# Sliding attention with a gated MLP on one core: values ahead of scores in one unit, gates, sums and applies in another order, and an end with all products copied by ScalarE

## The chip, the cores and the metric

The kernel runs on one core of one Trainium2 chip. The metric is the device time of one execution in microseconds (us). Three timed runs of the kernel before took 201.37, 201.47 and 202.03 us, with a median of 201.47.

## The reference: what is computed

```python
xn = _layernorm(x)                       # x: 1 x 2048 x 512, bf16
s  = _A_ref(xn, A_wqkv, A_wo)            # attention, then @ wo
g  = _silu(_B_ref(xn, w1, w2, w3, w4))   # MLP
return x + s * g
```

`_A_ref` is attention with 32 heads of 16 columns. Each position looks at 8 positions: itself and those 2, 4, ... 14 before it; positions before the start are masked. The softmax runs over these 8. `_B_ref` normalises, multiplies by `w1` (512x512), takes gelu, shifts the four quarters of the columns by -1, +1, -2 and +2 positions, multiplies by `w2`, adds its input, normalises again, and runs an MLP through 1376 columns (`w3`, gelu, `w4`) that is added as well.

## The kernel before

The 2048 positions are split into even and odd ones (`p` = 0, 1; 1024 each), since the attention only couples positions of the same parity. Everything is issued in an order written out by hand: `pin` keeps each instruction in program order on its engine, so each of TensorE (PE), VectorE (DVE), ScalarE (ACT) and SyncE (SP, which issues nearly all DMAs) works through its own list and waits at its head. Nothing is rescheduled.

**First part (until about 113 us).** Normalisation, q, k, v, `w1`, `w2`, and `w3` with gelu for four chunks of 512 positions. The results of `w3` stay in SBUF as `h3a` and `h3b`. The change touches nothing here.

**Second part: 18 units** (`for n in range(NU)`, line 843). A unit is 114 positions of one parity, in two blocks of 57. Units 0 to 8 are even positions, 9 to 17 odd ones. In unit `n` TensorE's list holds:

- `scores(n)` (line 584): 32 small matmuls of q against k into PSUM banks 0 to 3, then one exponential on ScalarE over 128x1824 elements (line 598), which writes the tile `prob`.
- `band(n - 1)` (line 600): VectorE zeroes by a minimum with a mask (line 603) what lies outside the 8 positions. From unit 15 on the band is that of unit `n` itself and stands later in the unit.
- `values(n - 2)` (line 608): 32 small matmuls of `prob` with v into bank 4 (`O_ps`, line 617) and 16 with `den_st` or `den_s2` into bank 5 for the softmax's denominators (`D_ps`, line 627); then ScalarE copies bank 4 into `oT` (line 632). From unit 16 on it is `values(n - 1)`, and unit 15 does both 13 and 14.
- a share of the 16 `w4` groups (`w4_take`, line 828; the matmuls are on line 729). A group is 128 positions and 11 matmuls; it holds one of a few free banks, and when its last matmul is issued, `done` puts the sum with the input on VectorE (line 742), which empties the bank, and appends a tanh for ScalarE (`tanhs`, line 749) and behind it a gate for VectorE (`gates`, line 751). For the tiles 13 to 15 the silu itself is taken on ScalarE (lines 745 and 740), without a gate. Tile 15 adds its input by an identity matmul (line 734).
- a small extra group: v for the odd positions in units 0 to 7 (`g_v`, line 758), and from unit 8 on one output tile (`g_fin`, line 770): four matmuls with `wo` (line 776), a copy on ScalarE (line 786), and, appended to `finals`, the multiply by the gate (line 790) and the sum with x (line 796) on VectorE. `stores` holds the writes to HBM.

The denominators are turned over in batches of units (0 to 3, 4 to 7, 8 to 11, 12 to 15, and 16 with 17). In units 5, 9, 13 and 16 (`ends`), `inverse` takes the reciprocal on VectorE (line 639), `write_rec` writes it to HBM by two DMAs on SyncE (line 648), one unit later `read_rec` reads it back spread over the heads (line 651), and two units after the reciprocal, or behind the loop for the fourth batch, `apply` multiplies `oT` by it on VectorE (line 664).

What stands where within a unit is set by the lines 851 to 893: the lists `finals`, `gates` and `tanhs` are emptied (`flush`) at fixed places between the three thirds of the unit's `w4` share.

**The end (lines 895 to 921).** `values(17)`, the last reciprocal, the last 8 matmuls of `w4`; then `expand` (line 666) spreads the last reciprocal over the heads by 8 matmuls into two banks, `keep_ps` copies them to SBUF on ScalarE (line 678, the "kept factors" `rk`), and `apply_kept` multiplies them into `oT` (line 684). Seven output tiles of the odd positions remain. Tiles 1 to 5 are copied by ScalarE; for tile 6 and the two halves of tile 7 VectorE multiplies straight out of PSUM (`act=False`, line 792). Tiles 1 to 5 are stored by SyncE, tile 6 and the first half of 7 by ScalarE's queue, and the second half by SyncE.

Of the kernel before, what the change touches and what calls it, by code (L numbers as in the profile page):

```python
# [20 lines left out]
def kernel(  # L21
# [17 lines left out]
    PE, DVE, ACT, POOL, SP = nc.tensor, nc.vector, nc.scalar, nc.gpsimd, nc.sync  # L39

    def pin(ins):

        return tc.keep_in_program_order(ins)
# [3 lines left out]
    D = 512  # L47
# [37 lines left out]
    def b4(shape, name):  # L85
        return sm4.tile(shape, BF16, name=name, tag="b4")
# [121 lines left out]
    class Norm:  # L208
# [22 lines left out]
        def apply(self, lo, hi):  # L231
            for j in range(lo, hi):
                pin(DVE.tensor_scalar(
                    out=self.dst[:, j, :], in0=self.src[:, j, :], scalar1=self.mv[:, j, 0:1],
                    scalar2=self.rstd[:, j : j + 1], op0=ALU.subtract, op1=ALU.mult,
                ))
# [347 lines left out]
    def scores(n):  # L584
        p, u = n // UP, n % UP
        for dt in range(ND):
            for k in range(2):
                b = 2 * u + k
                for rg in range(4):
                    r = slice(32 * rg, 32 * rg + 32)  # L590
                    pin(PE.matmul(  # L591
                        S_ps[:, rg, (2 * dt + k) * QB : (2 * dt + k + 1) * QB],
                        lhsT=kM[p][r, dt, b * QB + 1 : b * QB + 65, :].rearrange("p k e -> p (k e)"),
                        rhs=qT[p][r, dt, b * QB : (b + 1) * QB], start=True, stop=True,
                        tile_position=(32 * rg, 0),
                    ))
        pr = probs[n] = b4([P, 4, ND * NQ], "prob")
        pin(ACT.activation(pr, S_ps[:, :, 0 : ND * NQ], AF.Exp, scale=SCALE))  # L598

    def band(n):  # L600
        pr = probs[n]
        f = pr.rearrange("p r x -> p (r x)")
        pin(DVE.tensor_tensor(out=f, in0=f, in1=maskb[:], op=ALU.min))  # L603
        if n % UP == 0:
            z = pr[0:14].rearrange("p r (a k q) -> p (r a) k q", k=2, q=QB)
            pin(DVE.memset(z[:, :, 0, 0:7], 0.0))

    def values(n):
        p, u = n // UP, n % UP
        if u == 0:  # L610
            oT[p] = b8([P, ND, MQ], f"oT{p}")
        pr = probs.pop(n)
        for dt in range(ND):
            for k in range(2):
                for rg in range(4):
                    x = (2 * dt + k) * QB
                    pin(PE.matmul(  # L617
                        O_ps[32 * rg : 32 * rg + 32, x : x + QB],
                        lhsT=va_r[:, n % NV, k, 32 * (4 * dt + rg) : 32 * (4 * dt + rg) + 32],
                        rhs=pr[:, rg, x : x + QB], start=True, stop=True, tile_position=(0, 32 * rg),  # L620
                    ))
        b = batch_of[n]
        lo, hi = batches[b]
        st = den_st if hi - lo == 4 else den_s2
        for dt in range(ND):
            for rg in range(4):
                pin(PE.matmul(  # L627
                    D_ps[32 * rg : 32 * rg + 32, :], lhsT=st[:, 4 * (n - lo) + dt, :],
                    rhs=pr[:, rg, dt * NQ : (dt + 1) * NQ], start=(n == lo and dt == 0),
                    stop=(n == hi - 1 and dt == ND - 1), tile_position=(0, 32 * rg),  # L630
                ))
        pin(ACT.activation(
            oT[p][:, :, u * NQ : (u + 1) * NQ], O_ps[:, 0 : ND * NQ].rearrange("p (a q) -> p a q", q=NQ), AF.Copy
        ))
# [15 lines left out]
    def read_rec(b):  # L650
        pin(SP.dma_start(
            out=rr_t.rearrange("p j a q -> p (j a q)"),
            in_=ap_of(rec_ds[b][:], [[16 * NQ, 16], [0, 8], [1, 16 * NQ]]),
        ))
# [42 lines left out]
    tanhs, gates, vstores = [], [], []  # L697
# [72 lines left out]
    def g_fin(p, i, st=None, n=2, half=False, act=True, cols=None, later=None):  # L770

        c = slice(0, D) if cols is None else slice(*cols)
        W = c.stop - c.start

        def one(pt, dt):
            pin(PE.matmul(  # L776
                pt[:, 0:W], lhsT=oT[p][:, dt, i * P : (i + 1) * P], rhs=wo["sb"][:, dt, c],
                start=(dt == 0), stop=(dt == ND - 1),
            ))

        def done(pt):
            sg = fin.tile([P, D], BF16, name="sg", tag="f")[:, 0:W]
            pt = pt[:, 0:W]
            g = xn[p][:, i, c]
            if act:
                pin(ACT.activation(sg, pt, AF.Copy, scale=2.0 if half else 1.0))  # L786

            def steps():
                if act:
                    pin(DVE.tensor_tensor(out=sg, in0=sg, in1=g, op=ALU.mult))  # L790
                elif half:
                    pin(DVE.scalar_tensor_tensor(out=sg, in0=pt, scalar=2.0, in1=g, op0=ALU.mult, op1=ALU.mult))
                else:
                    pin(DVE.tensor_tensor(out=sg, in0=pt, in1=g, op=ALU.mult))
                x_o = xo[p][:, i, c]
                pin(DVE.tensor_tensor(out=x_o, in0=sg, in1=x_o, op=ALU.add))
                if cols is not None:
                    pin(st.dma_start(out=ov[p, i * P : (i + 1) * P, c], in_=x_o))
                elif st is not None:
                    stores.append((now["n"], lambda: store(st, p, i + 1 - n, n)))  # L800

            if later is None:
                steps()
            else:
                later.append(steps)

        return Group(ND, one, done)

    finals = []
# [8 lines left out]
    def flush(q):  # L818
        while q:
            q.pop(0)()  # L820

    def flush_stores(n):
        while stores and stores[0][0] <= n:
            stores.pop(0)[1]()
# [3 lines left out]
    def w4_take(k, extra=()):  # L828

        while k > 0 and open_w4:  # L830
            k -= open_w4[0].take(k)
            if open_w4[0].at == open_w4[0].n:
                open_w4.pop(0)
                if extra:
                    extra.pop(0).all()
# [5 lines left out]
    ends = {5: 0, 9: 1, 13: 2, 16: 3}  # L841
    load_va(0)
    for n in range(NU):
        now["n"] = n
        q = W4 * (n + 1) // NU - given
        given += q
        extra = small_g.get(n, [])
        if n == 0:
            w4_take(HEAD)

        if n - 1 in ends:
            read_rec(ends[n - 1])
        scores(n)
        if 1 <= n < 16:
            band(n - 1)
        if n >= 2:
            values(n - 2 if n < 16 else n - 1)
        if n + 1 < NU:
            load_va(n + 1)
        if n in xo_at:  # L860
            load_xo(*xo_at[n])
        if n == 4:
            load_wo()
        if n - 1 not in ends:
            flush_stores(n - 2)
        flush(vstores)
        flush(finals)
        if n in ends:
            recs[ends[n]] = inverse()
            write_rec(ends[n])  # L870
        if n == 17:
            free += [2, 3]
            pin(ACT.preload_act_table_set("silu_and_others"))
        w4_take(q // 3)
        if n < 15:
            flush(gates)
        flush(tanhs)
        if n == 15:
            apply(ends[n - 2])
        if n == 17:  # L880
            band(n)
        w4_take(q // 3, extra)
        if n < 15 and n - 2 in ends:
            apply(ends[n - 2])
        if 15 <= n < 17:
            band(n)
        if n == 15:
            values(14)
        w4_take(q - 2 * (q // 3), extra)
        if n >= 15:  # L890
            flush(gates)
        while extra:
            extra.pop(0).all()

    n = NU
# [4 lines left out]
    flush(gates)  # L900
    flush(tanhs)
    w4_take(LAST)
    banks = [PS[:, i, :] for i in range(2)]
    for j in range(2):
        expand(rec, NU - 2 + j, banks[j])
    kept = [keep_ps(b) for b in banks]
    flush(finals)
    g_fin(1, 1, SP).all()
    flush(tanhs)
    for j in range(2):  # L910
        apply_kept(NU - 2 + j, kept[j])
    g_fin(1, 2).all()
    g_fin(1, 3, SP).all()
    flush_stores(n)
    g_fin(1, 4).all()
    g_fin(1, 5, SP, half=True).all()
    flush_stores(n)
    g_fin(1, 6, ACT, 1, half=True, act=False).all()
    flush_stores(n)
    g_fin(1, 7, ACT, half=True, act=False, cols=(0, D // 2)).all()  # L920
    g_fin(1, 7, SP, half=True, act=False, cols=(D // 2, D)).all()


# [28 lines left out]
```

## Time and profile before

| | |
|---|---|
| timed runs, median | 201.47 us |
| the profiled execution, own time | 201.1 us |
| its span, first to last instruction | 199.3 us |
| TensorE matmul busy | 189.3 us (95%) |
| ScalarE busy | 128.5 us (64%) |
| VectorE busy | 117.9 us (59%) |
| GpSimd busy | 19.4 us (10%) |
| DMA, mean | 142 GB/s |
| granted TensorE clock, mean | 0.993 |

All durations come from the one profiled execution, whose own time is 1.8 us more than its span. In the timeline a line gives the start, the duration, the engine, the line of the kernel, the operation with what it writes and reads, and in brackets how long the engine had idled just before and what ended that. In the list of waits a line gives who waited for whom, with the total, the number of times and the longest. The chain of waits is followed back from the last instruction.

### The profile page before, as it was taken

Reading aid. Unit: us, or ns where it says so; the run is one execution under the profiler, and the core shown is the slowest. Engines: PE = TensorE matmul, PEld = TensorE weight load, DVE = VectorE, ACT = ScalarE, POOL = GpSimd, SP = SyncE. Lnnn points to the kernel's source line nnn. Section 1 sums busy time; section 2 is a strip of 40 time slices with the busy share of each in tenths; the row PEclk is TensorE's granted clock in tenths of the full one; section 3 lists DMA queues with packets and bytes.
Section 4 is the critical chain, followed back from the end, with each engine's and each line's share of the span. In section 5 each row is a group of like instructions: output and inputs, shape, how many; then the busy total and the mean of one; then the engine's idle time right before and its main releaser. Section 6 shows DMA issues by size and latency. Waiting matters only on the chain.

```text
span 199.3 us, 5290 instructions
## 1 busy us (share of the span) xinstructions
PE 189.3 (95%) x2285; PEld 92.0 (46%) x2285; DVE 117.9 (59%) x234; ACT 128.5 (64%) x143; POOL 19.4 (10%) x52
## 2 busy tenths in 40 slices
PE   7799999999999999999999999999999999999990
PEld 2464544554444444444444444554445445454540
DVE  7876785522076697585100034654769878796694
ACT  2188759558817615345564788687878868877850
POOL 1008058000002022015000000000000000000000
PEclk9999999999999999999999999999999999999997
DMA  5977655654000433853650062565944655762433
GB/s 129 369 239 240 216 119 209 221 174 135 0 0 3 132 83 105 210 107 106 149 170 0 0 187 79 166 193 151 268 134 122 166 167 150 175 188 71 146 105 105
DMA packets 33878, 28.37 MB, mean 142 GB/s; under 512 B 10808, under 2 KB 32832, under 8 KB 33856
## 3 DMA queue, kind: packets, MB, share of 16 engines
q1 hardware_dynamic: 33568, 27.84, 47.0%
q8 instruction: 18, 0.29, 0.6%
q10 hardware_dynamic: 288, 0.20, 0.3%
q14 instruction: 4, 0.03, 0.0%
HBM read 17.27 MB, written 8.67 MB: 130 GB/s over the span
## 4 chain that ended last, share of the span: by engine, by line
PE 79%; DVE 10%; ACT 4%; DMA 4%; issue 1%; SPq 0%; ACTq 0%; DVEq 0%
PE PS L442 19%; PE PS L301 17%; PE PS L729 16%; PE PS L776 7%; PE PS L400 4%; PE PS L335 4%; DMA ring<-rec_d 3%; ACT kM L327 3%; PE PS L617 3%; PE PS L591 2%; PE PS L760 2%; PE PS L291 2%; PE PS L627 2%; PE PS L283 1%; DVE l3s L219 1%; DVE xn L408 1%
## 5 line engine op out<-in xcount | busy, mean ns | idle before, releaser
L442 PE MATMUL PS<-x1nT,w_sb 128*128 128x512 bf16 (+1 forms) x176 | 38.3, 379 | 0.1
L598 ACT ACTIVATE prob<-PS 128x1824 bf16<-128x1824 f32 x18 | 30.4, 1688 | 5.4 <-PE PS L591 4.7
L729 PE MATMUL PS<-w_sb,h3a 128*128 128x512 bf16 x128 | 32.7, 380 | 0.7 <-DVE xn L742 0.7
L448 ACT ACTIVATE h3a<-PS 128x1024 bf16<-128x1024 f32 x16 | 16.4, 1023 | 20.9 <-PE PS L442 20.9
L742 DVE TENSOR_TENSOR xn<-PS,xn 128x512 bf16<-128x512 f32 x15 | 10.2, 680 | 30.7 <-PE PS L729 30.5
L442 PEld LDWEIGHTS <-w_sb 128*128 128x128 bf16 (+1 forms) x176 | 17.5, 100 | 20.8 <-DMA x1nT<-x1n_dram 0.6
L301 PE MATMUL PS<-xnT,wqk_sb 128*128 128x512 bf16 x112 | 25.0, 379 | 0.0
L327 ACT ACTIVATE kM<-PS,em 128x1024 bf16<-128x1024 f32 x16 | 20.6, 1401 | 3.7 <-PE PS L301 3.7
L603 DVE TENSOR_TENSOR prob<-prob,maskb 128x1824 bf16<-128x1824 bf16 x18 | 19.8, 1102 | 3.6 <-ACT prob L598 3.6
L408 DVE TENSOR_TENSOR xn<-PS,xn 128x1024 bf16<-128x1024 f32 x8 | 9.6, 1213 | 14.7 <-PE PS L400 14.7
L729 PEld LDWEIGHTS <-h3a 128*128 128x128 bf16 x128 | 11.3, 97 | 14.1 <-issue 1.9
L301 PEld LDWEIGHTS <-wqk_sb 128*128 128x128 bf16 x112 | 10.9, 98 | 12.7
L776 PE MATMUL PS<-wo_sb,oT 128*128 128x512 bf16 (+1 forms) x68 | 15.5, 366 | 0.0
L301 PE MATMUL PS<-xn2T,w_sb 128*128 128x512 bf16 x64 | 14.8, 379 | 0.1
L400 PE MATMUL PS<-w_sb,hT 128*128 128x512 bf16 x64 | 14.5, 379 | 0.1
L729 PE MATMUL PS<-w_sb,h3b 128*128 128x512 bf16 (+1 forms) x48 | 13.5, 381 | 0.0
L312 ACT ACTIVATE qT<-PS 128x1024 bf16<-128x1024 f32 x8 | 8.1, 1023 | 7.8 <-PE PS L301 7.7
L786 ACT ACTIVATE sg<-PS 128x512 bf16<-128x512 f32 x14 | 8.3, 596 | 6.2 <-PE PS L776 6.1
L346 ACT ACTIVATE vst<-PS 128x512 bf16<-128x512 f32 (+1 forms) x12 | 8.8, 744 | 3.5 <-ACT sig L749 2.4
L373 ACT ACTIVATE hT<-PS 128x1024 bf16<-128x1024 f32 x8 | 8.1, 1035 | 4.5 <-PE PS L301 4.5
L219 DVE BATCH_NORM_STATS2 l3s<-xn 128x6 f32<-128x512 bf16 x16 | 10.2, 682 | 0.2
L219 DVE BATCH_NORM_STATS2 l1s<-xn 128x6 f32<-128x512 bf16 x16 | 10.1, 677 | 0.0
(98 smaller groups left out, 225.7 us busy)
## 6 DMA issues: line engine op xcount, KB each, us to landing
ring<-v_d SPq DMA_DIRECT2D x18, 256.0 KB
v_d<-vst SPq DMA_DIRECT2D x16, 256.0 KB, 2.9
x1n_dram<-xn SPq DMA_DIRECT2D x4, 512.0 KB
xo<-in_A_x_dram SPq DMA_DIRECT2D x8, 256.0 KB, 4.0
ring<-rec_d SPq DMA_DIRECT2D x4, 456.0 KB, 5.2
out_dram<-xo SPq DMA_DIRECT2D x7, 256.0 KB, 3.1
xn<-in_A_x_dram SPq DMA_DIRECT2D x6, 256.0 KB, 4.1
w_sb<-in_B_w_dram SPq DMA_DIRECT2D x1, 1376.0 KB, 7.5
```

What stands on the lines that cost most here:

```text
L219: pin(DVE.bn_stats(out=self.st[:, j, :], in_=self.src[:, j, :]))
L301: pin(PE.matmul(pt[:, b, :], lhsT=w[:, dt, nt * P : (nt + 1) * P], rhs=rhs[:, dt, :], start=(dt == 0), stop=(dt == ND - 1),))
L327: pin(ACT.activation(kM[p][:, 2 * a : 2 * a + 2, 8 + k * CH : 8 + (k + 1) * CH, e], pt, AF.Copy, scale=em[:, e : e + 1]))
L400: pin(PE.matmul(pt[:, j, :], lhsT=w2_src(p, g, m0), rhs=w2_sb[:, g, :], start=(g == 0), stop=(g == ND - 1),))
L408: pin(DVE.tensor_tensor(out=xs, in0=pts[h], in1=xs, op=ALU.add))
L442: pin(PE.matmul(pt[:fs, ft % 2, :], lhsT=w3_sb[:, dt, ft * P : ft * P + fs], rhs=x1nT[:, dt, :], start=(dt == 0), stop=(dt == ND - 1),))
L448: pin(ACT.activation(t[:, o : o + 2, :], pt, AF.Gelu_apprx_tanh))
L598: pin(ACT.activation(pr, S_ps[:, :, 0 : ND * NQ], AF.Exp, scale=SCALE))
L603: pin(DVE.tensor_tensor(out=f, in0=f, in1=maskb[:], op=ALU.min))
L729: pin(PE.matmul(pt, lhsT=h3_of(c, ft)[:fs, jj * P : (jj + 1) * P], rhs=w4_sb[:fs, ft, :], start=(ft == 0), stop=(ft == NF - 1 and silu < 2),))
L742: pin(DVE.tensor_tensor(out=x_i, in0=pt, in1=x_i, op=ALU.add))
L776: pin(PE.matmul(pt[:, 0:W], lhsT=oT[p][:, dt, i * P : (i + 1) * P], rhs=wo["sb"][:, dt, c], start=(dt == 0), stop=(dt == ND - 1),))
```

## The change

In the loop over units:

- in unit 15 `values(13)` is issued ahead of `scores(15)`, no longer behind it;
- in unit 16 `finals` are emptied behind the second third and the band, no longer at the start of the unit;
- in units 0 to 14 the gates that were pending when the unit's first third is through are emptied behind the second third, no longer behind the first, and the `apply` of these units stands behind the last third, no longer ahead of it.

At the end:

- the silu of tile 15 (`flush(tanhs)`) comes ahead of the expansion and of the copies of the kept factors, no longer behind tile 1;
- the kept factors are applied ahead of output tile 1, no longer behind it;
- tile 6 and both halves of tile 7 are copied by ScalarE as the others are (`act` keeps its default), and the two halves' multiplies and sums are issued behind both copies;
- tile 6 and the first half of tile 7 are stored by SyncE, the second half by ScalarE's queue.

```diff
         if n - 1 in ends:
             read_rec(ends[n - 1])
+        if n == 15:
+            values(13)
         scores(n)
         if 1 <= n < 16:
             band(n - 1)
-        if n >= 2:
+        if n >= 2 and n != 15:
             values(n - 2 if n < 16 else n - 1)
...
         flush(vstores)
-        flush(finals)
+        if n != 16:
+            flush(finals)
         if n in ends:
             recs[ends[n]] = inverse()
             write_rec(ends[n])
...
         w4_take(q // 3)
-        if n < 15:
-            flush(gates)
+        late = list(gates)
+        gates.clear()
         flush(tanhs)
         if n == 15:
             apply(ends[n - 2])
         if n == 17:
             band(n)
         w4_take(q // 3, extra)
-        if n < 15 and n - 2 in ends:
-            apply(ends[n - 2])
+        if n < 15:
+            flush(late)
         if 15 <= n < 17:
             band(n)
+        if n == 16:
+            flush(finals)
         if n == 15:
             values(14)
         w4_take(q - 2 * (q // 3), extra)
+        if n < 15 and n - 2 in ends:
+            apply(ends[n - 2])
         if n >= 15:
+            flush(late)
             flush(gates)
...
     flush(gates)
     flush(tanhs)
     w4_take(LAST)
+    flush(tanhs)
     banks = [PS[:, i, :] for i in range(2)]
     for j in range(2):
         expand(rec, NU - 2 + j, banks[j])
     kept = [keep_ps(b) for b in banks]
     flush(finals)
-    g_fin(1, 1, SP).all()
-    flush(tanhs)
     for j in range(2):
         apply_kept(NU - 2 + j, kept[j])
-    g_fin(1, 2).all()
-    g_fin(1, 3, SP).all()
+    for i in range(1, 7):
+        g_fin(1, i, SP if i % 2 or i == 6 else None, 1 if i == 6 else 2, half=i >= 5).all()
+        if i != 6:
+            flush_stores(n)
+    g_fin(1, 7, SP, half=True, cols=(0, D // 2), later=finals).all()
+    g_fin(1, 7, ACT, half=True, cols=(D // 2, D), later=finals).all()
     flush_stores(n)
-    g_fin(1, 4).all()
-    g_fin(1, 5, SP, half=True).all()
-    flush_stores(n)
-    g_fin(1, 6, ACT, 1, half=True, act=False).all()
-    flush_stores(n)
-    g_fin(1, 7, ACT, half=True, act=False, cols=(0, D // 2)).all()
-    g_fin(1, 7, SP, half=True, act=False, cols=(D // 2, D)).all()
+    flush(finals)
```

## The prediction

> **What bounds the kernel now.** I read the page first, then TensorE's waits, then the order of time around each wait, and last the chain of waits at the end.
>
> The page, parts 1 and 2:
>
> ```profile
> span 199.3 us, 5290 instructions
> ...
> PE 189.3 (95%) x2285; PEld 92.0 (46%) x2285; DVE 117.9 (59%) x234; ACT 128.5 (64%) x143; POOL 19.4 (10%) x52
> ...
> PE   7799999999999999999999999999999999999990
> ...
> PEclk9999999999999999999999999999999999999997
> ```
>
> TensorE works through the whole span at the full clock; only the last slices, where nothing is left for it, are empty. So a microsecond counts if TensorE stood still in it, or if it lies behind TensorE's last matmul. All that the change touches runs after 133 us. TensorE's waits from 113 us on (us in total, times, longest):
>
> ```profile
> PE PS L729 <- DVE xn L742: 0.7, 3, 0.3
> PE PS L617 <- ACT oT L632: 0.5, 1, 0.5
> PE PS L617 <- issue: 0.2, 1, 0.2
> ```
>
> Five gaps, 1.44 us together. The timeline (start, duration, instruction, idle time before it) shows each from both sides. Unit 5 and unit 7:
>
> ```profile
> 133.96 0.87 DVE L639 RECIPROCAL rec<-PS 128x114 bf16<-128x114 f32 x1 [0.98 <-PE PS L627]
> 134.75 0.63 DVE L751 SCALAR_TENSOR_TENSOR xn<-sig,xn 128x512 bf16<-128x512 bf16 x1
> 135.29 0.68 DVE L742 TENSOR_TENSOR xn<-PS,xn 128x512 bf16<-128x512 f32 x1
> 136.02 1.24 PE L729 MATMUL PS<-w_sb,h3a 128*128 128x512 bf16 x5 [0.28 <-DVE xn L742]
> ...
> 143.19 1.11 DVE L664 TENSOR_TENSOR oT<-oT,ring 128x1824 bf16<-128x1824 bf16 x1 [1.29 <-DMA ring<-rec_d]
> 144.22 0.68 DVE L742 TENSOR_TENSOR xn<-PS,xn 128x512 bf16<-128x512 f32 x1
> 144.96 0.38 PE L729 MATMUL PS<-w_sb,h3a 128*128 128x512 bf16 x1 [0.22 <-DVE xn L742]
> ```
>
> L742 empties a PSUM bank that TensorE wants next. In unit 5 it stands on VectorE behind the gate (L751), in unit 7 behind the apply (L664); neither is needed soon. Unit 15, where ScalarE is the one that is late:
>
> ```profile
> 172.35 1.69 ACT L598 ACTIVATE prob<-PS 128x1824 bf16<-128x1824 f32 x1
> ...
> 173.92 0.56 ACT L632 ACTIVATE oT<-PS 128x456 bf16<-128x456 f32 x1
> ...
> 174.53 0.42 PE L617 MATMUL PS<-prob,ring 128*32 128x57 bf16 x32 [0.47 <-ACT oT L632]
> ```
>
> The copy of the products of unit 13 (L632) queues behind the whole exponential of unit 15 (L598), and the next values matmuls want the bank that it empties. Unit 16:
>
> ```profile
> 177.50 0.42 DVE L790 TENSOR_TENSOR sg<-sg,xn 128x512 bf16<-128x512 bf16 x1
> ...
> 178.30 0.86 DVE L639 RECIPROCAL rec<-PS 128x114 bf16<-128x114 f32 x1
> ...
> 179.76 1.24 PE L729 MATMUL PS<-w_sb,h3a 128*128 128x512 bf16 x5 [0.25 <-DVE xn L742]
> ```
>
> Here the finals (L790, L796) stand ahead of the reciprocal and L742. Last, the chain behind TensorE:
>
> ```profile
> 187.83 6.07 PE PS L776 x32
> ...
> 193.96 0.70 DVE sg L792
> 194.67 0.42 DVE xo L796
> ...
> 196.13 0.29 DVE xo L796
> ```
>
> TensorE's last product is ready at 193.90; VectorE ends at 196.42. In the timeline it has run without a gap since 189.36, where it had idled 0.77 us for ScalarE's copy of tile 1. So the tail is VectorE's.
>
> **The change, part by part.** Counts of instructions on TensorE and VectorE are unchanged; only their order and three forms differ.
>
> Unit 5: L742 goes ahead of L751. Its group's last matmul starts at 134.07 with three in 0.81, so it is done at 134.88, and VectorE is free at 134.75. L742 starts at 134.92, frees the bank at about 135.60; TensorE wanted it at 136.02 - 0.28 = 135.74. Gain **0.28**. L751 is 0.6 later and the band behind it 0.2; the gate is read by finals three units later, the band result a unit later.
>
> Unit 7: L664 goes behind L742. TensorE arrives 0.28 earlier, so L742 runs 143.63 to 144.31, and TensorE wants the bank at 144.96 - 0.22 - 0.28 = 144.46. Gain **0.22**. L664 then ends near 145.4; the first product that reads its output starts at 148.12, 147.6 after both shifts. In unit 11 the apply already stands behind L742; only L751 moves between them, and TensorE has no gap there. The gates and applies of the other units keep their order on VectorE: 0.
>
> Unit 15: the 48 small matmuls of values(13) run before scores(15). Their inputs are there: band(13) ended at 168.84, the oT copy of unit 12 at 170.68, TensorE arrives at 171.69. L632 starts at about 172.36, ahead of the exponential, and values(14) finds its bank free. Gain **0.47**. The price is that the exponential starts at 172.81 and not 172.35 (0.46 later). Behind it on ScalarE queue a tanh (174.35, now 174.5), the copy of unit 14 (175.02, now 175.05) and the products' copy, which TensorE's own arrival sets. Its reader, band(15), starts at 175.16 because two applies run on VectorE from 174.07 to 175.25; the exponential would now end at 174.50. Cover 0.66 us on VectorE, so nothing; values(15) want the band's result at 176.57 in the new schedule and have it at 176.26, so 0.3 is left there.
>
> Unit 16: without the finals ahead of it the reciprocal starts when the two gates end, at 177.47 instead of 178.30, in the old time of VectorE. L742 then runs 178.26 to 178.90 and TensorE, 0.47 earlier, wants the bank at 179.51 - 0.47 = 179.04. Gain **0.25**, with 0.1 to spare. The finals go behind band(16), into the wait of 1.63 us that VectorE has there for the next exponential. The reciprocal's two DMA writes and the read (L648, L651 on SyncE) go 0.8 earlier; the apply that waits for them (186.69, 0.39 on the DMA) is not what TensorE wants next.
>
> So TensorE ends 0.28 + 0.22 + 0.47 + 0.25 = **1.22** earlier.
>
> The tail, in the old times. ScalarE: the silu (L740) starts when its sum is ready, 187.47, the two factor copies (L678) at 187.97 and 188.50, the copy of tile 1 at 189.03, ready 189.63. In the old order the factor copies came first, then tile 1, then the silu. VectorE multiplies the kept factors (two L684, 190.16 to 190.78 before) inside its old gap of 0.77. Tile 1 starts at 189.64, not 189.36, but tile 2 follows 0.79 later instead of behind 0.62 of applies. With 0.79 for each pair L790, L796 (190.78, 191.23, 191.57 in the timeline), five pairs end at 193.61; tile 6's copy on ScalarE ends at 193.03 + 0.05 + 0.60 = 193.68, so its pair starts at 193.71, 0.25 sooner than before. Then the multiplies read SBUF, not PSUM: 0.45 + 0.34 for tile 6; for the half tiles, at the 0.29 of the 128x256 add, 0.31 + 0.21 and 0.31 + 0.29. That is 1.91 where the chain has 2.46. End 195.62 instead of 196.42: **0.80**. A 128x256 copy from PSUM on ScalarE is not in the trace. It lies between 0 and the 0.60 of 128x512; from that row and L632 (456 wide, 0.55) I estimate 0.39. Even at 0.60 the last one ends at 194.67, and VectorE asks for it at 195.03, so both ends cost 0.
>
> On this the Trainium skill speaks against the change: "VectorE: DVE Perf Modes", Rules for kernel authors, says to accept the slower PSUM source unless many operations will follow the copy, and here one multiply does. The trace has 0.68 against 0.42 for the multiply, and ScalarE idle; by the rule the copy would bring nothing, which is the second rival.
>
> Stores: tile 6 and the first half of tile 7 move from ScalarE's queue to SyncE's. SyncE waits 1.9 us before its last store, an issue takes 0.35 to 0.37, and the new issue times (193.7, 194.5, 195.1) are further apart: 0. The last store is issued by ScalarE at 195.62; its issue was 0.34 against 0.35 on SyncE. Its landing from that queue is not shown; between the 2.1 and the 3.1 of other stores, 0 to +1.0, and I take 0, the row of the same 64 KB. The fetch gap ("issue", 0.22) may vanish or appear elsewhere: -0.2 to +0.2, taken as 0.
>
> Sum: 1.22 + 0.80 = **2.02**. The profiled execution took 201.1 (span 199.3 and 1.8 around it), which gives 199.1. The three timed runs have a median of 201.47, 0.37 above; against those I forecast **199.4**.
>
> **The rivals.**
> 1. The waits come back one unit later. ScalarE is busy for 2.8 to 3.3 of each 4 us (busy time by stretch, 117 to 172 us), and the margins are 0.1 in unit 16 and 0.3 behind the later exponential. If both are missed, 0.25 + 0.47 are lost: 201.47 - 1.30 = **200.2**. Against it: VectorE's queue, not ScalarE, sets band(15).
> 2. The copies bring nothing: they take as long as the shorter multiplies save (0.55). The tail gains 0.25, in all 1.47: **200.0**. Against it: ScalarE does 0.60 a tile and TensorE 0.87.
> 3. The other side. A store on SyncE's queue moves only when the one before it has landed. Tiles 4 and 5 are issued at 193.7 - 1.2 = 192.5, then land one behind another: 3.1, 2.6 (128 KB, between its neighbours) and 2.1 give 200.3 where the old last store landed at 196.45 + 2.1 = 198.55. Slower by 1.7: **203.2**. It decides as soon as the half tile lands later than 198.55, so when the three together take over 6 us. Against it: the two writes of L648 in unit 5 are issued 134.86 and 135.57, and both have landed at 137.91, not 4 us after the first. The DMA engines are 76% busy from 195 to 196 and 63% in the next us, so a part of it may show. The Trainium skill ("DMA: Bandwidth & Descriptors", Issuing engines are not separate DMA queues) says that stores from either engine run on the same 16 engines and only issue time differs; by that the move costs nothing.
> 4. The order does not take effect, or gives back all that it gains. The instruction order of the changed kernel shows the moves on all three engines, which speaks against it: **201.4**.
>
> **How the numbers follow.** Forecast 0.60, its own spread 199.0 to 199.9 (the fetch gap, the landing); rival 1 0.20; rival 2 0.04; rival 3 0.10; rival 4 0.06. A measurement of this kernel tells 0.3%, 0.6 us, from no change. The first three cases are faster by more (0.84), rival 4 is within (0.06), rival 3 slower (0.10). The range 198.9 to 200.8 covers the forecast, rivals 1 and 2 and a late landing, and leaves out about 0.18.
>
> **What would show it.** TensorE's waits on L742 and L632 from 113 us on gone but for the fetch gap; L632 ahead of L598 in unit 15; finals behind the band in unit 16; VectorE's 0.77 gap filled by L684; last VectorE instruction about 2.0 earlier, 1.7 us behind TensorE's last matmul instead of 2.5. Wrong would be a new TensorE wait on L603 in unit 16, a bank wait in the tail, or an end that lies more than 3 us behind the last VectorE instruction (2.9 now).

## The result, and the profile after

The changed kernel took 199.31 us (median of 4 runs, 198.96 to 199.51) beside 201.42 for the kernel before: a ratio of 0.9888, 95% interval 0.9863 to 0.9914, 2.1 us faster where 2.0 were forecast. Run again beside the last experiments it took 198.76 against 201.09, 0.9887 (0.9871 to 0.9903).

The page of the changed kernel, span and first part:

```profile
span 197.8 us, 5263 instructions
...
PE 185.3 (94%) x2254; PEld 91.8 (46%) x2285; DVE 118.1 (60%) x234; ACT 129.7 (66%) x146; POOL 19.6 (10%) x52
```

The span is 1.5 shorter, not 2.1: this execution (199.51) is the slowest of its four, and the profiled one of the kernel before (201.1) was below its median. TensorE's waits from 113 us on (in total, times, longest):

```profile
PE PS L729 <- issue: 2.4, 15, 0.2
PE PS L617 <- issue: 0.6, 1, 0.6
```

The waits on L742 and L632 are gone. The first line is an artefact: the page counts 2254 matmuls for 2285 weight loads, and where a matmul's record is missing its 0.22 us look like a wait of 0.16. (e1 below has the same loop with all 2285 records, and its unit 5 takes 3.89 us from scores to scores, as it does here.) The second line is real: a gap for want of instructions, 0.22 before and 0.62 now. I call it the fetch gap.

The timeline at the four places (start, duration, instruction, idle time before it):

```profile
135.06 0.69 DVE L742 TENSOR_TENSOR xn<-PS,xn 128x512 bf16<-128x512 f32 x1
...
135.80 1.24 PE L729 MATMUL PS<-w_sb,h3a 128*128 128x512 bf16 x5
...
143.72 0.69 DVE L742 TENSOR_TENSOR xn<-PS,xn 128x512 bf16<-128x512 f32 x1 [2.03 <-PE PS L729]
144.33 1.10 DVE L664 TENSOR_TENSOR oT<-oT,ring 128x1824 bf16<-128x1824 bf16 x1
144.46 0.38 PE L729 MATMUL PS<-w_sb,h3a 128*128 128x512 bf16 x1
...
172.25 0.54 ACT L632 ACTIVATE oT<-PS 128x456 bf16<-128x456 f32 x1
...
172.68 1.70 ACT L598 ACTIVATE prob<-PS 128x1824 bf16<-128x1824 f32 x1
...
173.89 0.42 PE L617 MATMUL PS<-prob,ring 128*32 128x57 bf16 x32
...
178.25 0.69 DVE L742 TENSOR_TENSOR xn<-PS,xn 128x512 bf16<-128x512 f32 x1
...
178.99 1.24 PE L729 MATMUL PS<-w_sb,h3a 128*128 128x512 bf16 x5
```

Each L742 now starts when its group ends, L632 goes ahead of the exponential, and none of the TensorE lines has an idle time. The chain of waits at the end:

```profile
188.18 0.50 ACT sg L786
...
188.70 0.44 DVE sg L790
...
193.79 0.21 DVE sg L790
...
194.56 0.29 DVE xo L796
```

TensorE's last 32 matmuls run from 186.90 to 193.12, VectorE ends at 194.85: 1.73 behind, where it was 2.53. Between 188.70 and the end the chain is VectorE's alone.

### The profile page after: what moved, and what is told of

Read it like the earlier page. It is cut to its first block, busy times and chain, and to the rows that moved or that the text cites. A ratio compares the mean times of both kernels' runs of the same rounds, so it can differ in the third digit from the quotient of the medians.

```text
span 197.8 us, 5263 instructions
## 1 busy us (share of the span) xinstructions
PE 185.3 (94%) x2254; PEld 91.8 (46%) x2285; DVE 118.1 (60%) x234; ACT 129.7 (66%) x146; POOL 19.6 (10%) x52
## 4 chain that ended last, share of the span: by engine, by line
PE 76%; DVE 11%; DMA 4%; ACT 4%; issue 3%; POOL 1%; another core or an unknown queue 0%; SPq 0%; DVEq 0%
PE PS L442 19%; PE PS L729 19%; PE PS L301 13%; PE PS L776 4%; PE PS L335 4%; PE PS L760 3%; PE PS L617 3%; PE PS L591 3%; PE PS L400 3%; ACT kM L327 3%; DMA x1nT<-x1n_dram 2%; PE PS L291 2%; PE PS L627 2%; DVE sg L790 2%; DVE xo L796 2%
## 5 line engine op out<-in xcount | busy, mean ns | idle before, releaser
L729 PE MATMUL PS<-w_sb,h3a 128*128 128x512 bf16 x113 | 29.5, 379 | 1.8 <-issue 1.6
L742 DVE TENSOR_TENSOR xn<-PS,xn 128x512 bf16<-128x512 f32 x15 | 10.3, 687 | 32.6 <-PE PS L729 32.3
L603 DVE TENSOR_TENSOR prob<-prob,maskb 128x1824 bf16<-128x1824 bf16 x18 | 19.8, 1102 | 2.1 <-ACT prob L598 2.1
L729 PEld LDWEIGHTS <-h3a 128*128 128x128 bf16 x128 | 11.3, 97 | 13.4 <-issue 1.2
L786 ACT ACTIVATE sg<-PS 128x512 bf16<-128x512 f32 (+1 forms) x17 | 9.6, 572 | 6.5 <-PE PS L776 6.5
L729 PE MATMUL PS<-w_sb,h3b 128*128 128x512 bf16 (+1 forms) x44 | 12.8, 380 | 0.8 <-issue 0.8
```

The costliest lines, as they stand in the source:

```text
L729: pin(PE.matmul(pt, lhsT=h3_of(c, ft)[:fs, jj * P : (jj + 1) * P], rhs=w4_sb[:fs, ft, :], start=(ft == 0), stop=(ft == NF - 1 and silu < 2),))
L742: pin(DVE.tensor_tensor(out=x_i, in0=pt, in1=x_i, op=ALU.add))
```

## The experiments

The first four are parts of the change, timed in five rounds beside the kernel before; the others start from the changed kernel, but for e8. The table has what is read from each timing and profile:

- the ratio to the kernel before with its interval;
- the fetch gap as the list of waits names it, in unit 12 where nothing else is said;
- what unit 12 lost: the time from its first scores matmul to that of unit 13, less the 3.89 us that this takes where no gap stands there;
- the packet: the time from TensorE's weight load at place 2997 of its list to the start of the next packet of instructions (16 KB on the instruction queue, in the trace's DMA records). Places count TensorE's weight loads and matmuls from the start, one each; the gap in unit 12 stands at place 3253, 256 behind 2997;
- the DMA engines' share from 159 to 160 us as the profile counts it, which can come out over 1;
- the start of the last 32 matmuls, and VectorE's end behind the last of them (the tail).

| run | ratio | gap | unit 12 lost | packet | DMA share | last 32 start | tail |
|---|---|---|---|---|---|---|---|
| before | 1 | 0.22 | 0.40 | 1.07 | 0.86 | 187.67 | 2.53 |
| changed | 0.9888 | 0.62 | 0.79 | 1.42 | 0.55 | 186.90 | 1.73 |
| e1, loop only | 0.9917 (0.9894 to 0.9941) | 0.34 | 0.52 | 1.20 | 0.28 | 186.40 | 2.52 |
| e2, end only | 0.9957 (0.9942 to 0.9972) | 0.41 | 0.59 | 1.08 | 0.73 | 187.80 | 1.80 |
| e3, unit 15 only | 0.9979 (0.9963 to 0.9996) | 0.67 | 0.84 | 1.38 | 0.66 | 187.71 | 2.52 |
| e4, gates and applies | 0.9975 (0.9958 to 0.9993) | none | 0.06 | 0.57 | 0.10 | 186.72 | 2.53 |
| e5, no copies | 0.9925 (0.9906 to 0.9944) | 0.53 | 0.70 | 1.32 | 0.36 | 186.63 | 2.19 |
| e6, old stores | 0.9913 (0.9895 to 0.9931) | none | 0.30 | 0.88 | 0.24 | 186.22 | 1.73 |
| e7, changed, list moved on | 0.9903 (0.9886 to 0.9920) | 0.25 in unit 16 | 0 | | | 186.38 | 1.72 |
| e8, before, list moved on | 0.9996 (0.9981 to 1.0011) | 0.22 in unit 16 | 0 | | | 187.53 | 2.52 |
| e9, second read | 0.9901 (0.9885 to 0.9916) | 0.77 | 0.94 | 1.26 | 1.08 | 186.85 | 1.73 |
| e10, quarter of the read | 0.9865 (0.9850 to 0.9880) | none | 0 | 0.10 | 0.08 | 185.71 | 1.73 |
| e11, sums on GpSimd | 0.9920 (0.9906 to 0.9935) | 0.61 in unit 16 | 0 | | | 186.47 | 2.66 |
| e12, changed again | 0.9887 (0.9871 to 0.9903) | none | 0.14 | 0.82 | 0.19 | 186.07 | 1.73 |

"none" says that the list names no gap; e6 and e12 still lost 0.30 and 0.14 there, inside a group of matmuls that it shows as one.

**e1: the changed loop with the old end.**

> The changed loop with the old end. My theory: the three TensorE waits on L742 and the one on L632 are gone, and the gap for want of instructions in unit 12 is 0.4 longer than before, as in the changed kernel; TensorE's last matmul ends 0.8 earlier than before (193.1), the tail behind it stays 2.5 long, the time falls by 0.8 to 1.2 us against before. Rival (the loop gives nothing that lasts, all of it is the end): no change within 0.3. Rival (the waits add in full): 1.2 or more.

0.83% or 1.7 us (1.2 to 2.1) faster, and the waits on L742 and L632 gone. The rival that the waits add in full has it; I had counted on the long gap in unit 12, and here it was 0.34. The tail is the old one.

**e2: the old loop with the changed end.**

> The old loop with the changed end. My theory: all five TensorE gaps as before (1.44 us), last matmul at 193.9 as before, VectorE ends 1.7 behind it and not 2.5; 0.8 us faster than before. Rival (the end only gains because TensorE comes earlier): no change. Rival (the end gives the whole gain): 2.0 faster.

0.9 us faster (0.6 to 1.2), with the last 32 matmuls 0.1 later. Four of the five gaps of before are in its loop; the one in unit 7 is not named (more on it at the end), so "all five" was wrong. The end's gain needs nothing of the loop, and the two together (1.26%) are the change's 1.12% within the intervals.

**e3: only the new place of values(13).**

```diff
+        if n == 15:
+            values(13)
         scores(n)
...
-        if n >= 2:
+        if n >= 2 and n != 15:
```

> Only values(13) ahead of scores(15), all else as before. My theory: TensorE's wait on L632 (0.47) is gone, the exponential of unit 15 starts 0.46 later and nothing waits for it, the wait on L742 in unit 16 (0.25) grows, since the finals still stand ahead of the reciprocal there while TensorE comes earlier: a gain of 0.2 to 0.5 us. Rival (the later exponential comes back as a wait on L603 in unit 16): no gain, a new TensorE wait on L603 of 0.3 or more.

0.4 us faster (0.1 to 0.7). The timeline has one line that shows why unit 16's reorder belongs with it:

```profile
179.80 1.02 PE L729 MATMUL PS<-w_sb,h3a 128*128 128x512 bf16 x4 [0.48 <-DVE xn L742]
```

TensorE comes 0.5 earlier, and 0.2 of it is lost again at the reciprocal that still stands behind the finals (the wait is 0.25 before, 0.48 here). No wait on L603 appears.

**e4: only the gates and applies of units 0 to 14.**

```diff
-        if n < 15:
-            flush(gates)
+        late = list(gates)
+        gates.clear()
         flush(tanhs)
...
+        if n < 15:
+            flush(late)
...
+        if n < 15 and n - 2 in ends:
+            apply(ends[n - 2])
```

> Only the gates and applies of units 0 to 14 moved. My theory: the waits on L742 in units 5 and 7 (0.28 and 0.22) are gone, and the gap for want of instructions in unit 12 (0.22 before) grows by 0.3 to 0.4, since that instruction block does not come earlier: a lasting gain of only 0.1 to 0.2 us. Rival (both gaps last to the end): 0.5 us faster and the gap in unit 12 at 0.22.

0.5 us faster (0.1 to 0.8), the rival's number. TensorE's waits of this kernel:

```profile
PE PS L617 <- ACT oT L632: 0.5, 1, 0.5
PE PS L729 <- DVE xn L742: 0.3, 1, 0.3
```

Only unit 15's and unit 16's waits are left. The gap in unit 12, which I expected to grow, is not named, and unit 12 lost 0.06. It is thus no fixed price; in the eleven profiles that have it in unit 12 or nowhere (all but e7, e8 and e11) it is not named four times and otherwise between 0.22 and 0.77, and unit 12 lost between 0 and 0.94.

**e5: the changed kernel without the three copies on ScalarE.**

```diff
-        g_fin(1, i, SP if i % 2 or i == 6 else None, 1 if i == 6 else 2, half=i >= 5).all()
+        g_fin(1, i, SP if i % 2 or i == 6 else None, 1 if i == 6 else 2, half=i >= 5, act=i != 6).all()
...
-    g_fin(1, 7, SP, half=True, cols=(0, D // 2), later=finals).all()
+    g_fin(1, 7, SP, half=True, act=False, cols=(0, D // 2), later=finals).all()
```

(and the same for the second half, on ScalarE's queue)

> The changed kernel, but VectorE multiplies tile 6 and the halves of tile 7 straight out of PSUM, as before the change. My theory: these three multiplies go back from 0.42, 0.28 and 0.28 to 0.68, 0.42 and 0.42, so VectorE ends 0.5 later (195.4, not 194.85), 0.5 us slower than the changed kernel, the loop's gain and the earlier kept factors unchanged. Rival (the copies on ScalarE bring nothing, their own time takes up the saving): the same as the changed kernel.

By the profile the copies are worth 0.46: the tail is 2.19 and not 1.73, and tile 6's multiply is again

```profile
192.58 0.68 DVE L792 SCALAR_TENSOR_TENSOR sg<-PS,xn 128x512 bf16<-128x512 f32 x1
```

The timing doesn't tell the two apart. The nearest kernel timed in the same rounds is e6, which has the copies: 199.59 against 199.31, 0.3 slower where I expected 0.5, with intervals that overlap, and the fetch gap varies by as much as the difference. So the price of the copies rests on the profile.

**e6: the changed kernel with the stores on their old queues.**

```diff
-        g_fin(1, i, SP if i % 2 or i == 6 else None, 1 if i == 6 else 2, half=i >= 5).all()
+        g_fin(1, i, ACT if i == 6 else SP if i % 2 else None, 1 if i == 6 else 2, half=i >= 5).all()
...
-    g_fin(1, 7, SP, half=True, cols=(0, D // 2), later=finals).all()
-    g_fin(1, 7, ACT, half=True, cols=(D // 2, D), later=finals).all()
+    g_fin(1, 7, ACT, half=True, cols=(0, D // 2), later=finals).all()
+    g_fin(1, 7, SP, half=True, cols=(D // 2, D), later=finals).all()
```

> The changed kernel with the stores of tile 6 and of tile 7's first half on ScalarE's queue and the second half on SyncE's, as before the change. My theory: no change against the changed kernel within 0.2 us; issue takes 0.35 to 0.37 from either, and the end lies 2.9 behind VectorE's last instruction in both. Rival (stores on one queue wait for each other): faster than the changed kernel by 0.3 or more, with less than 2.9 between VectorE's last instruction and the end.

No difference. VectorE ends at 194.17 and the span at 197.1, 2.9 later; in the changed kernel 194.85 and 197.8, 2.9 as well.

**e7 and e8: TensorE's list moved on by 100 places**, in the changed kernel and in the kernel before.

```diff
+    for i in range(50):
+        r = slice(32 * (i % 4), 32 * (i % 4) + 32)
+        pin(PE.matmul(
+            PS[r, 6, 0:16], lhsT=ones_bf[:, 0:32], rhs=ones_bf[:, 0:16],
+            start=True, stop=True, tile_position=(0, 32 * (i % 4)),
+        ))
```

> The changed kernel with 50 tiny matmuls (16 columns) more among the warm-up matmuls, where TensorE is idle for 0.9 us: they move every later TensorE instruction 100 places down its list. My theory: TensorE's list arrives in blocks of 256 instructions (16 KB packets of the instruction queue), and the block border in unit 12 comes 3.5 us behind the one before it while a read of rec_d fills the DMA engines; with the border elsewhere the gaps for want of instructions in unit 12 (0.62) and in scores(16) (0.2) are gone, at most 0.4 comes back at the start: 0.4 to 0.8 us faster than the changed kernel. Rival (the gap belongs to that place: a bank or a semaphore that the trace does not name): the gap stays in unit 12 at 0.6 and the time does not fall.

> The kernel before with the same 50 tiny matmuls. My theory: only its 0.22 gap in unit 12 goes, so it gains 0 to 0.2 us, less than the changed kernel does by the same edit; the four waits on L742 and L632 stay. Rival (the edit speeds or slows the start by itself): both kernels move by the same amount.

The gap left unit 12 in both, so it doesn't belong to that place in the work. It belongs to a place in the list: in unit 12 it stands at place 3253, and in e7, e8 and e11, which all have the 50 matmuls more, a gap of 0.25, 0.22 and 0.61 stands in unit 16 at place 4273. That is 1020 places behind, four short of four times 256, by a count that has no other instructions. But the time did not fall as I expected: 0.9903 is not below the changed kernel's 0.9887 to 0.9888 from other rounds, and beside e6 in the same rounds (199.31) e7 is 0.4 lower (198.94), with intervals that overlap. Besides the gap at its new border there is one wait, on the reader that the prediction's first rival names:

```profile
173.34 1.18 DVE L671 TENSOR_TENSOR oT<-oT,ring 128x456 bf16<-128x456 bf16 x2 [0.51 <-DMA ring<-rec_d]
...
175.68 0.42 PE L624 MATMUL PS<-prob,ring 128*32 128x57 bf16 x32 [0.25 <-DVE prob L610]
```

The edit adds seven lines, so L624 is L617, L610 is L603 and L671 is L664. The band of unit 15 is 0.25 late, but not for the later exponential, which ended at 173.33: the two applies ahead of the band on VectorE waited 0.51 for the read of `rec_d`. In e10 and e11, where TensorE is at this place within 0.06 us of the same time and the applies don't wait, there is no such wait. e8 did not move (0.9996), as I expected, but of the four waits on L742 and L632 three stay: the one in unit 7 is gone.

**e9: a second read of `rec_d` in unit 10; e10: a quarter of the first one.**

```diff
+    rr_2 = const.tile([P, 16 * NQ], BF16, name="rr_2")
...
         if n - 1 in ends:
             read_rec(ends[n - 1])
+            if n == 10:
+                pin(SP.dma_start(
+                    out=rr_2, in_=ap_of(rec_ds[1][:], [[16 * NQ, 16], [0, 8], [1, 16 * NQ]])
+                ))
```

```diff
+        w = 4 * NQ if b == 1 else 16 * NQ
...
-            out=rr_t.rearrange("p j a q -> p (j a q)"),
-            in_=ap_of(rec_ds[b][:], [[16 * NQ, 16], [0, 8], [1, 16 * NQ]]),
+            out=rr_t.rearrange("p j a q -> p (j a q)")[:, 0:w],
+            in_=ap_of(rec_ds[b][:], [[16 * NQ, 16], [0, 8], [1, w]]),
```

> The changed kernel with a second, equal read of the second batch's rec_d behind the first one in unit 10, into a tile that nothing reads. My theory: the block of instructions that unit 12 wants comes late because the DMA engines are filled by the first read (98% busy from 157 to 160 us in the trace before); with twice the load the gap for want of instructions near 160 us grows to 1 us or more in the profile, and the time rises by 0.5 to 3 us against the changed kernel. Rival (the gap is a matter of the instruction stream alone, whatever the DMA engines do): the gap stays between 0 and 0.7 and the time does not move.

> The changed kernel, but the read of the second batch's rec_d fetches only a quarter of each row, so three of its four units are scaled by values left from the first batch. My theory: no gap for want of instructions near 160 us, and 0 to 0.6 us faster than the changed kernel. Rival (the instruction stream alone): the gap appears as before, 0.3 on the mean, and the time does not move.

With the second read the gap is the largest of all profiles,

```profile
160.47 0.34 PE L618 MATMUL PS<-prob,ring 128*32 128x57 bf16 x21 [0.77 <-issue]
```

but not the 1 us or more that I expected, and the time is 0.3 us over the changed kernel beside it (e12; 199.10 and 198.76), inside the intervals. With a quarter of the read there is none, and the time is 0.4 lower (198.35), again with intervals that overlap. e9 and e10 themselves differ by 0.75 us, and their intervals (0.9885 to 0.9916, 0.9850 to 0.9880) do not meet: with more of `rec_d` read there the kernel takes longer. In the two profiles TensorE differs by 1.14 at the last 32 matmuls, 0.94 of it in unit 12 and 0.2 in scores(16). One profile without a gap would prove little by itself, since e12 is nearly without one as well.

**e11: two sums on GpSimd**, on top of e7.

```diff
-    def g_fin(p, i, st=None, n=2, half=False, act=True, cols=None, later=None):
+    def g_fin(p, i, st=None, n=2, half=False, act=True, cols=None, later=None, add=DVE):
...
-                pin(DVE.tensor_tensor(out=x_o, in0=sg, in1=x_o, op=ALU.add))
+                pin(add.tensor_tensor(out=x_o, in0=sg, in1=x_o, op=ALU.add))
...
-        g_fin(1, i, SP if i % 2 or i == 6 else None, 1 if i == 6 else 2, half=i >= 5).all()
+        g_fin(1, i, SP if i % 2 or i == 6 else None, 1 if i == 6 else 2, half=i >= 5, add=POOL if i in (2, 4) else DVE).all()
```

> The changed kernel with the 50 tiny matmuls at the start and with the last sums of output tiles 2 and 4 on GpSimd in place of VectorE. My theory: the end is VectorE's, so each sum taken off it brings the end 0.34 sooner until the copies on ScalarE set it (VectorE's last instruction then about 1.1 behind TensorE's last matmul, not 1.7): 0.4 to 0.6 us faster than the changed kernel with the tiny matmuls alone. Rival (a sum of 128x512 takes GpSimd so long, or holds VectorE up so much, that the stores of tiles 2 to 5 end last): the same or slower.

The rival was right: 0.9920 beside 0.9903 for e7, and nothing gained. The timeline:

```profile
189.65 1.15 POOL L803 TENSOR_TENSOR xo<-sg,xo 128x512 bf16<-128x512 bf16 x1 [95.39 <-DVE sg L797]
189.95 1.13 DVE L797 TENSOR_TENSOR sg<-sg,xn 128x512 bf16<-128x512 bf16 x1 [0.44 <-ACT sg L793]
```

A sum takes GpSimd 1.15 us, and the multiply that VectorE starts meanwhile takes 1.13 instead of 0.42 and ends 0.28 behind it. The tail grew from 1.72 to 2.66. The Trainium skill ("SBUF — State Buffer", SBUF: two separate sides) has GpSimd and a VectorE operation with two SBUF inputs lock each other out of a shared port; the 1.13 agrees.

**e12: the changed kernel again.**

> The changed kernel once more, on the same chip as the three others. My theory: 2.0 to 2.3 us faster than the kernel before; the gap for want of instructions near 160 us lies between 0 and 0.7 in its profile, other than 0.62, because it differs from one execution to the next. Rival (the gap is fixed): 0.62 again.

0.9887, and no gap named in its profile (the 32 matmuls of that place take 0.57 in place of 0.42, so 0.15 at most). No version that does all the work beat the changed kernel beyond its interval.

## Why the prediction was right, point by point

- **Units 5 and 7 (0.28 and 0.22).** Right in mechanism: both waits gone, the gate and the apply later without a reader that minds. e4 has these two alone at 0.5 (0.1 to 0.8). But unit 7's term is no fixed price. The apply (L664) that held L742 up waits itself for the read of `rec_d`; with the old order it starts at 143.19 in the kernel before, 143.14 in e2, 143.10 in e3 and 142.70 in e8, and unit 7 lost 0.30, 0.08, 0.17 and nothing. The 0.22 was one execution's.
- **Unit 15 (0.47).** Right in place and order: L632 at 172.25 (forecast 172.36) and the exponential at 172.68 (172.81). Nothing waits for the later exponential in any profile. VectorE's queue sets band(15), as the prediction said against its first rival; the one wait on the band, in e7, came from applies that waited for a read.
- **Unit 16 (0.25).** Right, and bound to unit 15: alone, unit 15's move raises this wait to 0.48 (e3).
- **The sum of the loop (1.22).** The four places are right, and each is a little undersized. From the first scores matmul of a unit to that of the next or next but one, in the kernel before and in e6, which has the changed loop and no fetch gap in unit 16:

| | before | e6 | less | forecast |
|---|---|---|---|---|
| unit 5 | 4.25 | 3.89 | 0.36 | 0.28 |
| unit 7 | 4.19 | 3.89 | 0.30 | 0.22 |
| units 14 and 15 | 8.82 | 8.29 | 0.53 | 0.47 |
| unit 16 | 4.23 | 3.89 | 0.34 | 0.25 |

  Together that is 1.53. The forecast took the idle time in brackets, which counts from the end of the last matmul. The trace models that end 0.38 us behind the start, while the matmuls of a row start 0.22 apart, so a part of each wait is not in the brackets. Unit 5 shows it; from these rows to the next L729 (136.02 and 135.80) it is 1.30 before and 0.94 now, 0.36 less, where the bracket says 0.28:

```profile
134.72 1.03 PE L760 MATMUL PS<-wv_sb,xnT 128*128 128x512 bf16 x4
```

```profile
134.86 1.03 PE L760 MATMUL PS<-wv_sb,xnT 128*128 128x512 bf16 x4
```

- **The tail (0.80).** Right to the last digit in the trace: 2.53 to 1.73. The kept factors fill VectorE's gap, the multiplies from SBUF take 0.43, 0.28 and 0.28, and ScalarE's copy of 128x256 takes 0.38 (estimated 0.39). e5 prices the copies at 0.46 (forecast 0.55, less 0.07 because tile 6's copy is ready that much after the pair before it), e2 the whole end at 0.9 (0.6 to 1.2).
- **The rule against the copies.** The Trainium skill ("VectorE: DVE Perf Modes", Rules for kernel authors) would keep the PSUM source where one operation follows. Here VectorE was the engine that ended last and ScalarE had room, and by the profile the copies paid. The measurement decides.
- **The stores (0).** Right (e6). The rival in which one queue serves a store at a time is out.
- **The fetch gap (0, from -0.2 to +0.2).** Here the size was off: unit 12 lost from nothing to 0.94 from one profile to the next. In the profiled execution of the changed kernel it took back 0.4, and 0.2 more in scores(16), where 32 matmuls took 0.61 instead of 0.40; a further 0.14 is a later start of the units. That is why this profile shows TensorE only 0.77 earlier.

So the loop's terms are 0.3 too small, and the fetch gap, taken as nothing, took a part of that back. That the measured 2.1 and 2.3 us lie so near the forecast 2.02 is in part luck: e10, which lost nothing at these borders, is 2.7 us faster, which is 1.53 and 0.80 and the 0.40 that unit 12 of the kernel before lost.

What sets the gap can be followed one step. That it is a border in the instruction list, 256 places from the next, is shown by e7, e8 and e11. In the ten profiles that lost time in unit 12, TensorE goes on 2.7 to 3.0 us after the packet of instructions starts, so what differs is when that packet starts: 0.10 us behind place 2997 in e10, 0.57 to 1.42 in the others, and with few exceptions the later it starts the more is lost. (The share from 159 to 160 us parts the same profiles, with a gap named at 0.28 and more and none at 0.24 and less, but does not order them: 0.40 is lost at 0.86, and 0.79 at 0.55.) That the amount read from `rec_d` changes the time is shown by e9 beside e10; that it does so by holding this packet up is supported by their two profiles (1.26 and 0.10). It is not that read alone: in unit 16 of e7, e8 and e11 the packet starts about 2 us behind the border before, with the DMA engines' share at 0.77 or more in each us from 173 to 176, and in e7 the read of `rec_d` had landed by 173.34. What decides between 0.57 and 1.42 stays open: the DMA engines' share from 157 to 158 us is 0.97 or more in all ten (0.52 in e10).

## What to carry to other kernels

Where one engine is busy nearly all the time, look for each of its few waits, and ask which instruction in the releasing engine's list could have stood behind the one that releases it; such moves add up, and cost nothing while the moved one's reader is far away. A move that lets the busy engine come earlier can expose the next wait (unit 16 behind unit 15), so they are priced together. Price a wait by the starts of instructions on both sides of it, over several profiles: the idle time in brackets came out 0.1 short here, and one wait of the four was there in one profile and gone in another. In a tail, count the time of the engine that ends last and hand its slower forms to an engine that has room; ScalarE was one here, GpSimd was not, since its sums stretched VectorE's multiplies from 0.42 to 1.13 us.

## What the runs showed of the hardware

TensorE's instructions arrive in packets of 16 KB: the page of the kernel before counts 18 of them (0.29 MB) for 4570 weight loads and matmuls, about 256 each. At a border TensorE stood still for up to 0.77 us, and lost up to 0.94, when 256 instructions passed in about 3.5 us (in the changed kernel from 156.4 to 159.9) beside a read that filled the DMA engines. The Trainium skill ("Runtime: NRT & Kernel Launch", Instruction fetch mechanics) has the blocks of 16 KiB and calls the crossing mostly hidden; in this kernel it was not, in seven of the eleven profiles that have this border in unit 12. That accounts for the spread that the profiles of one order of work show at the start of the last 32 matmuls: 186.07 (e12), 186.22 (e6) and 186.90 (changed) with 0.35, 0.30 and 1.00 lost at the two borders in unit 12 and scores(16), which leaves 185.72, 185.92 and 185.90.
